# One unit of attention work made of 128 tokens from each of four sequences instead of 512 tokens in a row

## The chip, the core and the metric

One core of one Trainium2 chip runs the whole program. The metric is the device time of one execution in microseconds (us); lower is better. The engines are named as the profile names them: PE (matrix multiply), PEld (its weight load), DVE (vector), ACT (scalar), POOL (GpSimd) and SP, which issues the DMAs.

## What is computed

Three stages follow one another: a linear attention with a decaying state, and two feed-forward layers. Of the reference, what matters:

```python
B, H, S, D = 4, 8, 768, 48
state = zeros(B, H, D, D)
for t in range(S):
    state = alpha[:, :, t, :, None] * state + einsum('bhd,bhe->bhde', k[:, :, t], v[:, :, t])
    y[:, :, t] = einsum('bhd,bhde->bhe', q[:, :, t], state)
x = y.transpose(0, 2, 1, 3).reshape(3072, 384)
h = x @ w_in;  x = (h * cos(h)) @ w_out                      # d_ff 2048
h = max(x @ w1, x @ w2, x @ w3);  out = h @ w_out2           # d_ff 768
```

## The kernel before

**Tiling.** The 3072 tokens (four sequences of 768, one behind the other) are cut into NU = 6 units of HB = 512 tokens in a row, so a unit is two thirds of a sequence and a sequence begins at chunk 0 of units 0 and 3 and at chunk 4 of units 1 and 4. A unit has NC = 8 chunks of C = 64 tokens. The eight heads go in NP = 4 pairs; the pair's two heads lie on partitions 0 to 47 and 64 to 111 (PR = 112 rows). One call of `att` does one unit of one pair; there are 24 calls. All 24 are called attentions here, for short.

**One attention.** Two scans on DVE make the decays inside each chunk (`g`, L370 and L380) and their inverse form (`al`, L376 and L385). In the first unit a scan's second input lies in PSUM, in the later units in SBUF. Two POOL multiplies scale keys and queries (L372 or L384, and L387). PE transposes the keys (L392) and ACT copies them (L395). PE then multiplies keys with queries (L404) and keys with values (L409) into two PSUM banks `r`, one for even and one for odd chunks. The scores are masked into `a`: in the first unit by an ACT copy (L416) and a POOL multiply (L417), later by one DVE instruction (L420). The state goes through the unit's chunks one after the other on DVE: L428 computes state times decay plus the chunk's key-value product, on a 112x48 tile, once for each chunk; where a sequence begins L426 copies instead. The scaled states `d` that the queries need are made by POOL for all 8 chunks together (L440, one instruction for each of the pair's heads); in the first unit ACT makes those of one head, one chunk at a time (L435). PE then adds up the outputs in `values`: L453 multiplies scores with values in 64x64 tiles, and L459 multiplies scaled states with queries, two matmuls for each chunk on 112 rows and 48 columns; chunks that begin a sequence need none. `d` holds zeros outside the head's own rows, which the program writes once at the start (L638). ACT copies the output to the `xt` or `yy` tile (L474), and its low part follows (L477 and L479 in the first unit, L481 later).

**The layers.** `moe1` (L501 to L530) is the first layer: for each unit 16 blocks f, of which each needs 9 matmuls of 128x512 with `wi` (L501 to L503), an element-wise chain through `q` on ACT, DVE and POOL (L508 to L523), and 9 matmuls with `wo` (L528 to L530). Its weights come by DMA once, during the first unit: 32 blocks, each of which takes three DVE instructions (L315 to L317), an ACT copy (L320) and a POOL subtraction (L321). The second layer (L579 to L604) follows when the first has ended.

**What sets the order.** The order of all instructions is computed when the program is built: `Program.order` is a list scheduler with a duration for each operation, a due time, and a lag between engines; each engine then runs its own list in that order, in sequence. Operations marked `port=True` and all of POOL's are kept apart in the plan. PSUM has five shared banks, whose use the scheduler also assigns. Two engines that read one PSUM bank are put in the order in which the program states them.

## Time and profile before

| | |
|---|---|
| timed runs | 815.31, 817.70, 818.28 us; median 817.7 us |
| profiled execution, first to last instruction | 815.2 us, mean granted PE clock 0.985 |
| instructions | 15114 |
| PE busy | 791.5 us, 97% |
| DVE busy | 476.4 us, 58% |
| ACT busy | 360.9 us, 44% |
| POOL busy | 192.8 us, 24% |

The profiled execution's time outside its span is not given apart; its span lies 0.1 us under the lowest timed run and 2.5 us under the median. The shares are means over stages that differ: in the first 60 us all engines work on the first unit's attentions and on weights, from there to about 140 us the weights still arrive while the first unit's layer runs, and from then on PE alone is full. A busy share of PE says nothing on its clock: the granted clock stands beside it in the views by time. It was 1.00, full speed at 2.4 GHz, in most of the run, and 0.5, which is 1.2 GHz, in parts of the first 60 us.

### The profile page before, as it was taken

The page shows a single profiled execution, that of the slowest core. Times are in us where ns is not written, and L with a number is a line of the kernel's source. Part 1 is how long each engine was busy: PE and PEld are TensorE (multiplying, and loading weights), DVE is VectorE, ACT ScalarE, POOL GpSimd, SP SyncE. Part 2 cuts the span into 40 slices and gives each one's busy share as a digit, 9 for nine tenths or more (in the row PEclk, how much of TensorE's full clock was granted, in tenths as well). Part 3 has the DMA queues.
Part 4 walks back from the last instruction along what each step waited for, and adds up shares of the span by engine and source line. Part 5 has one row for each costly group of instructions (what it writes and reads, how often), then busy time and mean ns, then how long its engine had stood idle before and what let it go on. Part 6 is the DMA issues. An engine that isn't in the chain of part 4 may idle for free.

```text
span 815.2 us, 15114 instructions
## 1 busy us (share of the span) xinstructions
PE 791.5 (97%) x6168; PEld 646.0 (79%) x6168; DVE 476.4 (58%) x924; ACT 360.9 (44%) x667; POOL 192.8 (24%) x191
## 2 busy tenths in 40 slices
PE   7679999999999999999999999999999999999998
PEld 6567778888878878888888788888888888888886
DVE  7988999765786587667679955452232222322221
ACT  4575655555645565555577746531121121112121
POOL 7777876530231023101123200110000000000000
PEclk8789999999999999999999999999999999999999
DMA  9745564430242033103135600412020020200001
GB/s 273 214 132 174 182 209 141 130 93 5 88 147 54 2 115 108 43 1 108 34 107 161 221 23 1 156 58 86 26 83 27 14 91 26 78 27 13 14 27 39
DMA packets 26661, 71.86 MB, mean 88 GB/s; under 512 B 3488, under 2 KB 3488, under 8 KB 26592
## 3 DMA queue, kind: packets, MB, share of 16 engines
q1 hardware_dynamic: 26592, 70.90, 26.9%
q8 instruction: 48, 0.79, 0.4%
q14 instruction: 21, 0.17, 0.1%
HBM read 54.37 MB, written 14.16 MB: 84 GB/s over the span
## 4 chain that ended last, share of the span: by engine, by line
PE 84%; DVE 6%; POOL 4%; issue 2%; DMA 2%; ACT 2%; SPq 0%; POOLq 0%; DVEq 0%; ACTq 0%
PE ps L580 9%; PE ps L579 9%; PE ps L581 9%; PE acc L528 7%; PE ps L501 7%; PE acc L530 7%; PE acc L529 7%; PE ps L503 7%; PE ps L502 7%; PE ps L603 3%; PE ps L602 3%; PE ps L604 3%; PE ps L459 2%; PE ps L404 1%; PE ps L453 1%
## 5 line engine op out<-in xcount | busy, mean ns | idle before, releaser
L501 PE MATMUL ps<-xt,wih 128*128 128x512 f32 x288 | 116.3, 404 | 3.7 <-ACT kt L395 2.2
L528 PE MATMUL acc<-gh,woh 128*128 128x512 f32 x288 | 116.5, 405 | 0.7 <-DVE yy L538 0.5
L530 PE MATMUL acc<-gl,woh 128*128 128x512 f32 x288 | 112.8, 392 | 0.5 <-DVE gl L523 0.4
L502 PE MATMUL ps<-xt,wih 128*128 128x512 f32 x288 | 113.2, 393 | 0.0
L503 PE MATMUL ps<-xt,wil 128*128 128x512 f32 x288 | 113.0, 392 | 0.0
L529 PE MATMUL acc<-gh,wol 128*128 128x512 f32 x288 | 112.4, 390 | 0.0
L517 DVE SCALAR_TENSOR_TENSOR ps<-q,ps 128x512 f32<-128x512 f32 x76 | 52.7, 694 | 56.9 <-ACT q L511 56.7
L589 DVE TENSOR_TENSOR ps<-t,ps 128x512 f32<-128x512 f32 x36 | 25.0, 696 | 103.6 <-PE ps L581 103.5
L510 ACT ACTIVATE q<-q 128x512 f32<-128x512 f32 x96 | 60.5, 631 | 52.3 <-DVE q L509 52.0
L508 ACT ACTIVATE q<-ps 128x512 int32<-128x512 f32 x96 | 57.1, 595 | 57.0 <-PE ps L503 54.6
L509 DVE SCALAR_TENSOR_TENSOR q<-q,ps 128x512 f32<-128x512 int32 x96 | 65.7, 685 | 21.1 <-ACT q L508 20.8
L590 ACT ACTIVATE h<-ps 128x512 fp32r<-128x512 f32 x36 | 21.5, 598 | 112.1 <-DVE ps L589 112.0
L523 DVE TENSOR_TENSOR gl<-ps,gh 128x512 fp32r<-128x512 f32 x76 | 52.1, 686 | 26.7 <-PE ps L503 15.9
L501 PEld LDWEIGHTS ps<-xt,wih 128*128 128x128 f32 x288 | 54.7, 190 | 16.4 <-ACT kt L395 3.2
L440 POOL TENSOR_TENSOR d<-s,g 48x384 f32<-48x384 f32 x44 | 37.0, 842 | 125.5 <-DVE s L428 123.7
L587 DVE TENSOR_TENSOR t<-t,ps 128x512 f32<-128x512 f32 x36 | 24.8, 688 | 71.2 <-PE ps L581 70.4
L528 PEld LDWEIGHTS acc<-gh,woh 128*128 128x128 f32 x288 | 54.0, 188 | 14.9 <-DVE yy L538 2.3
L518 ACT ACTIVATE gh<-ps 128x512 fp32r<-128x512 f32 x76 | 45.4, 598 | 44.0 <-DVE ps L517 41.5
L530 PEld LDWEIGHTS acc<-gl,woh 128*128 128x128 f32 x288 | 54.1, 188 | 13.5 <-DVE gl L523 1.4
L503 PEld LDWEIGHTS ps<-xt,wil 128*128 128x128 f32 x288 | 54.7, 190 | 11.8
L502 PEld LDWEIGHTS ps<-xt,wih 128*128 128x128 f32 x288 | 54.9, 190 | 10.4
L529 PEld LDWEIGHTS acc<-gh,wol 128*128 128x128 f32 x288 | 54.1, 188 | 9.9
(122 smaller groups left out, 1579.4 us busy)
## 6 DMA issues: line engine op xcount, KB each, us to landing
raw<-in_wt SPq DMA_DIRECT2D x56, 384.0 KB, 3.3
kq<-in_qka SPq DMA_DIRECT2D x23, 448.0 KB, 4.2
x1d<-yy SPq DMA_DIRECT2D x18, 512.0 KB, 2.6
xt<-x1d SPq DMA_DIRECT2D x18, 512.0 KB, 4.4
v<-in_vv SPq DMA_DIRECT2D x22, 256.0 KB, 3.2
al<-in_qka SPq DMA_DIRECT2D x24, 228.4 KB, 2.7
outT<-y SPq DMA_DIRECT2D x18, 256.0 KB, 2.0
xt<-yy SPq DMA_DIRECT2D x36, 64.0 KB, 2.6
```

The source lines that it names most:

```text
L501: pe.matmul(ps, wi["h"][:, f, cc], xt[:, cc, 0], start=(cc == 0), stop=False)
L502: pe.matmul(ps, wi["h"][:, f, cc], xt[:, cc, 1], start=False, stop=False)
L503: pe.matmul(ps, wi["l"][:, f, cc], xt[:, cc, 0], start=False, stop=(cc == NR - 1))
L508: op("Act", act(HB, True), lambda: se.activation(q.bitcast(I32), ps, AF.Copy, scale=INV2PI), [hk], [qk], m)
L509: op("DVE", dve(HB), lambda: ve.scalar_tensor_tensor(q, q.bitcast(I32), -TWOPI, ps, ALU.mult, ALU.add), [hk], [qk], m)
L510: op("Act", act(HB), lambda: se.activation(q, q, AF.Sin, scale=0.5), (), [qk], m)
L528: pe.matmul(acc[c], oh, gh, start=(f == 0), stop=False)
L529: pe.matmul(acc[c], ol, gh, start=False, stop=False)
L530: pe.matmul(acc[c], oh, gl, start=False, stop=(f == NF1 - 1))
L579: pe.matmul(ps, w2t["h"][m][:, f, cc], xt[:, cc, 0], start=(cc == 0), stop=False)
L580: pe.matmul(ps, w2t["h"][m][:, f, cc], xt[:, cc, 1], start=False, stop=False)
L581: pe.matmul(ps, w2t["l"][m][:, f, cc], xt[:, cc, 0], start=False, stop=(cc == NR - 1))
```

## The change

A unit now holds 128 tokens of each of the four sequences, two chunks of each. The host arranges the inputs and the output for that; the arrays keep their shapes. Chunk c of a unit is chunk h = c % 2 of sequence i = c // 2, so the even bank of `r` holds all four sequences' first chunks and the odd bank all second ones. The state of a pair is one tile 112x(4x48) and takes two steps in a unit instead of eight. Every sequence begins in unit 0.

New names and lines (of the changed kernel): POOL multiplies the old states of all four sequences by the first chunk's decay into `d[:, 0]` (L421, not in unit 0); DVE adds the key-value products (L422), multiplies by the second chunk's decay into `d[:, 1]` (L423; in unit 0 L425 multiplies the key-value products straight from PSUM) and adds the second products (L430). `d` has no zeros any more. ACT copies half of the rows of each `d` into a new tile `z` (L428), whose other rows are zero from the start (L626). In `values` the matmul L446 takes the place of L459: in a first pass (x = 0) one head's 48 rows of `d` and of the queries alone, in a second (x = 1) the 112 rows of `z`. The old L426, L428, L435 and L440 are gone.

```diff
-    s_b = [ap.tile([PR, NC, D], F32, name=f"s{p}") for p in range(NP)]
-    d_b = [ap.tile([PR, 2, NC, D], F32, name=f"d{i}") for i in range(2)]
+    s_b = [ap.tile([PR, N2, D], F32, name=f"s{p}") for p in range(NP)]
+    d_b = [ap.tile([PR, 2, N2, D], F32, name=f"d{i}") for i in range(2)]
+    z_b = [ap.tile([PR, 2, N2, D], F32, name=f"z{i}") for i in range(2)]
...
-        for c in range(NC - 1):
-            op("DVE", 0.2, lambda c=c: state(c), [rk[c % 2], *kgs, (*sk, c)], [(*sk, c + 1)], t0 + 0.25)
...
+        kvs = [r[h][0:PR, 0:AO].rearrange("p (b e) -> p b e", b=N2) for h in range(2)]
+        gs = [g.rearrange("p (b h) t -> p b h t", h=2)[:, :, h, 0:1].to_broadcast([PR, N2, D]) for h in range(2)]
+        if u:
+            op("Pool", pool(N2 * D), lambda: ge.tensor_tensor(d[:, 0], s, gs[0], ALU.mult), [*kgs, sk], [(dk, 0)], t0 + 0.2)
+            op("DVE", dve(N2 * D), lambda: ve.tensor_tensor(s, kvs[0], d[:, 0], ALU.add), [rk[0], (dk, 0)], [sk], t0 + 0.25)
+            op("DVE", dve(N2 * D), lambda: ve.tensor_tensor(d[:, 1], s, gs[1], ALU.mult), [*kgs, sk], [(dk, 1)], t0 + 0.25, port=True)
+        else:
+            op("DVE", dve(N2 * D), lambda: ve.tensor_tensor(d[:, 1], kvs[0], gs[1], ALU.mult), [rk[0], *kgs], [(dk, 1)], t0 + 0.25)
+        for h in range(0 if u else 1, 2):
+            w = slice(UP * (1 - h), UP * (1 - h) + D)
+            op("Act", act(N2 * D), lambda h=h, w=w: se.activation(z[w, h], d[w, h], AF.Copy), [(dk, h)], [("z", n2, h)], t0 + 0.25)
+        if u + 1 < NU:
+            op("DVE", dve(N2 * D), lambda: ve.tensor_tensor(s, kvs[1], d[:, 1], ALU.add), [rk[1], (dk, 1)], [sk], t0 + 0.27)
...
-            for c in range(NC):
-                if not firsts[c]:
+            for x in range(2):
+                for i in range(N2):
                     for j in range(2):
-                        h = c % 2
-                        pe.matmul(y[h][UP * j:UP * j + D, c // 2 * C:(c // 2 + 1) * C], d[:, j, c], qv3[:, c], start=False, stop=False, skip_group_check=True)
...
+                        h, w = (j + x) % 2, slice(UP * j, UP * j + D)
+                        dd, qq = (z[:, h, i], qv3[:, 2 * i + h]) if x else (d[w, h, i], qv3[w, 2 * i + h])
+                        if u or h:
+                            pe.matmul(y[h][w, i * C:(i + 1) * C], dd, qq, start=False, stop=False, skip_group_check=True)
...
-            for t in (*s_b, *d_b):
+            for t in z_b:
                 ge.memset(t, 0.0)
```

The order of the lists moves with it, at three places that matter here.

DVE, first unit, before. The rows run from the third attention's last scan (`al_109`) through the state steps of the first two attentions (`s_125`, `s_122`) to the first weight block (`raw_92`) and the first step of the third attention (`s_123`):

```order
L376 SCALAR_TENSOR_TENSOR al_109<-al_109,acc_97 112x260
L426 COPY s_122<-ps_98 112x48
L428 SCALAR_TENSOR_TENSOR s_122<-s_122,g_114,ps_102 112x48
L428 SCALAR_TENSOR_TENSOR s_122<-s_122,g_114,ps_98 112x48
L428 SCALAR_TENSOR_TENSOR s_125<-s_125,g_113,ps_100 112x48
...
L315 TENSOR_SCALAR ps_99<-raw_92 128x384
L316 SCALAR_TENSOR_TENSOR ps_99<-raw_92,ps_99 128x384
L317 SCALAR_TENSOR_TENSOR raw_92<-raw_92,ps_99 128x384
L428 SCALAR_TENSOR_TENSOR s_122<-s_122,g_114,ps_102 112x48
L426 COPY s_123<-ps_100 112x48
```

The same engine and place in the changed kernel, where L371 is the scan and L311 to L313 are the weight block:

```order
L371 SCALAR_TENSOR_TENSOR al_109<-al_109,acc_97 112x260
L425 TENSOR_TENSOR d_126<-ps_101,g_115 112x192
L311 TENSOR_SCALAR ps_98<-raw_92 128x384
L430 TENSOR_TENSOR s_123<-ps_99,d_126 112x192
L312 SCALAR_TENSOR_TENSOR ps_98<-raw_92,ps_98 128x384
L313 SCALAR_TENSOR_TENSOR raw_92<-raw_92,ps_98 128x384
```

The third attention's state product now stands straight behind its last scan and ahead of the first weight block.

POOL, before, the work ahead of the first two `gl` (L515), which the first L528 needs; `kq_110` is the second unit's third attention, `d_126` its first, `wil` a weight block:

```order
L384 TENSOR_TENSOR kq_110<-kq_110,g_113 112x512
L440 TENSOR_TENSOR d_126<-s_125,g_114 48x384 x2
L387 TENSOR_TENSOR kq_110<-kq_110,al_107 112x512
L321 TENSOR_TENSOR wil<-raw_94,wih 128x384
L515 TENSOR_TENSOR gl_88<-q_83,gh_86 128x512
L515 TENSOR_TENSOR gl_89<-q_84,gh_87 128x512
```

And in the changed kernel (L379, L382 and L503 are the same operations as L384, L387 and L515):

```order
L379 TENSOR_TENSOR kq_110<-kq_110,g_113 112x512
L382 TENSOR_TENSOR kq_110<-kq_110,al_107 112x512
L421 TENSOR_TENSOR d_126<-s_123,g_113 112x192
L503 TENSOR_TENSOR gl_88<-q_83,gh_86 128x512
L503 TENSOR_TENSOR gl_89<-q_84,gh_87 128x512
```

No weight block stands right ahead of the first `gl` any more, and where two products of 48x384 for the first attention stood there is one of 112x192 for the third.

PE, one output block of a later unit, before (L453 the scores' part, L459 the states' part, L501 the layer's next matmul):

```order
L453 MATMUL ps_101<-a_120,v_116 64x64 x2
L453 MATMUL ps_99<-a_120,v_116 64x64 x2
L459 MATMUL ps_101<-kq_111,d_126 48x64 x2
L459 MATMUL ps_99<-kq_111,d_126 48x64 x2
...
L501 MATMUL ps_98<-xt_1844,wih 128x512
```

And in the changed kernel (L446 the states' part, first with `d`, then with `z`; L489 the layer's next matmul):

```order
L446 MATMUL ps_99<-kq_110,d_127 48x64
L446 MATMUL ps_100<-kq_110,d_127 48x64
...
L446 MATMUL ps_100<-kq_110,z_129 48x64
L446 MATMUL ps_99<-kq_110,z_129 48x64
...
L489 MATMUL ps_101<-xt_881,wih 128x512
```

There are 16 matmuls of L446 in each block of units 1 to 5, eight with `d`, whose successive matmuls change bank and rows each time, then eight with `z`; L459 had 16, or 14 where a sequence begins. In unit 0 L446 has eight.

## Rows read from the trace of the kernel before

**Rows 1.** The page, part 1: busy us of each engine; part 2: granted clock by slices

```profile
PE 791.5 (97%) x6168; PEld 646.0 (79%) x6168; DVE 476.4 (58%) x924; ACT 360.9 (44%) x667; POOL 192.8 (24%) x191
PEclk8789999999999999999999999999999999999999
```

**Rows 2.** Busy time by stretch: stretch, length, PE, PEld, DVE, ACT, POOL, clock, DMA

```profile
0.00:20.00 20.00, 15.28 (x298) 13.91 (x298) 15.64 (x43) 9.12 (x26) 15.57 (x27) 0.83 0.94 273
20.00:40.00 20.00, 14.01 (x264) 11.11 (x263) 17.90 (x42) 11.64 (x35) 15.44 (x15) 0.75 0.72 216
40.00:60.00 20.00, 15.26 (x168) 11.95 (x169) 17.35 (x37) 13.28 (x26) 15.53 (x14) 0.83 0.40 128
60.00:80.00 20.00, 19.67 (x173) 14.97 (x173) 17.98 (x41) 11.87 (x24) 14.84 (x13) 1.00 0.60 187
80.00:100.00 20.00, 18.82 (x224) 15.41 (x219) 19.28 (x43) 13.01 (x27) 18.04 (x15) 1.00 0.57 175
100.00:120.00 20.00, 18.02 (x195) 13.95 (x193) 19.88 (x44) 12.04 (x25) 15.95 (x14) 1.00 0.63 195
200.00:400.00 200.00, 200.00 (x2102) 162.00 (x2094) 141.18 (x286) 112.47 (x201) 39.60 (x40) 1.00 0.23 71
```

**Rows 3.** Timeline of PE, three places: start us, us, instruction; the group count of L459

```profile
164.41 0.69 PE L404 MATMUL ps<-kq 48*64 48x64 f32 x32
164.93 0.62 PE L409 MATMUL ps<-v,kt 64*64 64x48 f32 x32
...
207.40 0.69 PE L453 MATMUL ps<-a,v 64*64 64x64 f32 x32
208.03 0.99 PE L459 MATMUL ps<-kq,d 112*48 112x64 f32 x28
208.95 0.50 PE L501 MATMUL ps<-xt,wih 128*128 128x512 f32 x1
...
161.11 1.10 PE L459 MATMUL ps<-kq,d 112*48 112x64 f32 x32
162.14 0.50 PE L501 MATMUL ps<-xt,wih 128*128 128x512 f32 x1
...
L459 PE MATMUL ps<-kq,d 112*48 112x64 f32 x592 | 20.7, 222 | 0.0
```

**Rows 4.** Groups by line; the first two of 10.3 to 49 and 49 to 130 us

```profile
L428 DVE SCALAR_TENSOR_TENSOR s<-s,g,ps 112x48 f32<-112x48 f32 x34 | 8.5, 255 | 1.7 <-ACT a L416 1.4
L428 DVE SCALAR_TENSOR_TENSOR s<-s,g,ps 112x48 f32<-112x48 f32 x29 | 7.5, 257 | 0.2
L420 DVE TENSOR_TENSOR a<-ps,tri 128x256 f32<-128x256 f32 x40 | 15.4, 417 | 3.0 <-PE ps L409 3.0
L435 ACT ACTIVATE d<-s,g 48x48 f32<-48x48 f32 x28 | 9.0, 332 | 2.1 <-DVE s L428 1.4 <-DVE s L426 0.4
L474 ACT ACTIVATE xt<-ps 128x256 fp32r<-128x256 f32 x30 | 10.3, 377 | 7.3 <-PE ps L459 7.2
```

**Rows 5.** Timeline of DVE and PE in the first 60 us, single rows

```profile
14.33 0.69 DVE L376 TENSOR_TENSOR_SCAN al<-al,acc 112x260 f32<-112x260 f32 x1
17.40 0.56 DVE L315 TENSOR_SCALAR ps<-raw 128x384 uint32<-128x384 uint32 x1 [0.36 <-DMA raw<-in_wt]
18.84 0.97 PE L409 MATMUL ps<-q,kt 64*64 64x48 f32 x32
48.95 0.69 DVE L509 SCALAR_TENSOR_TENSOR q<-q,ps 128x512 f32<-128x512 int32 x1 [0.30 <-ACT q L508]
59.88 0.50 PE L528 MATMUL acc<-gh,woh 128*128 128x512 f32 x1
```

**Rows 6.** One line's instructions: shortest, median, longest ns; POOL's products as a group

```profile
L385 DVE TENSOR_TENSOR_SCAN al<-al,inv x20: 1227/1241/2422, 35.7 to 367.5; 112x520 f32<-112x520 f32 x20
L387 POOL TENSOR_TENSOR kq<-kq,al x23: 1173/1194/2102, 6.8 to 373.8; 112x512 f32<-112x512 f32 x23
L440 POOL TENSOR_TENSOR d<-s,g 48x384 f32<-48x384 f32 x44 | 37.0, 842 | 125.5 <-DVE s L428 123.7
```

More of the change, by code (lines that the diff above doesn't have):

```diff
@@ L359, in att @@
         kg, ik, tk, dk, sk = ("g", m % NGS), ("iv", n2), ("kt", n2), ("d", n2), ("s", p)
-        firsts = [(u * NC + c) % CPB == 0 for c in range(NC)]
         op("SP", HW, lambda: nc.sync.dma_start(t, qka[u, p, :, 0:KO]), (), [kf], t0 - 4, dma(PR * KO * 4))
@@ L421, in att @@
                    [rk[j], "tri"], [("a", n2, j)], t0 + 0.2)
-        def state(c):
-            o, kvc = s[:, (c + 1) % NC], r[c % 2][0:PR, c // 2 * D:(c // 2 + 1) * D]
-            if firsts[c]:
-                ve.tensor_copy(o, kvc)
-            else:
-                ve.scalar_tensor_tensor(o, s[:, c], g[:, c, 0:1], kvc, ALU.mult, ALU.add)
-        for c in range(NC - 1):
-            op("DVE", 0.2, lambda c=c: state(c), [rk[c % 2], *kgs, (*sk, c)], [(*sk, c + 1)], t0 + 0.25)
-            if u < DAC and not firsts[c + 1]:
-                for j in range(DAH):
-                    w = slice(UP * j, UP * j + D)
-                    op("Act", act(D) + 0.21, lambda c=c, j=j, w=w: se.activation(d[w, j, c + 1], s[w, c + 1], AF.Copy, scale=g[w, c + 1, 0:1]),
-                       [*kgs, (*sk, c + 1)], [(dk, j, c + 1)], t0 + 0.25)
@@ L437, in att @@
-        for j in range(2):
-            if u >= DAC or j >= DAH:
-                w = slice(UP * j, UP * j + D)
-                op("Pool", pool(NC * D), lambda j=j, w=w: ge.tensor_tensor(d[w, j], s[w], g[w, :, 0:1].to_broadcast([D, NC, D]), ALU.mult),
-                   [*kgs, *[(*sk, c) for c in range(NC)]], [(dk, j, c) for c in range(NC)], t0 + 0.25)
-            elif not firsts[0]:
-                w = slice(UP * j, UP * j + D)
-                op("Act", act(D) + 0.21, lambda j=j, w=w: se.activation(d[w, j, 0], s[w, 0], AF.Copy, scale=g[w, 0, 0:1]), [*kgs, (*sk, 0)], [(dk, j, 0)], t0 + 0.25)
@@ L709, in heads @@
     def heads(a):
[L711 to L712 removed]
+        a = _np.asarray(a).reshape(B, NP, 2, NU, 2, C, D)
+        return a.transpose(3, 1, 2, 6, 0, 4, 5).reshape(NU, NP, 2, D, NC, C)
     al, q, k = heads(inputs["alpha"]), heads(inputs["q"]), heads(inputs["k"])
```

21 lines of the change are left out of this document (8 added, 13 removed).

## The prediction

> **What bounds the kernel now.** I read the page first: PE is busy 97% of the span [rows 1], so the question is where the last 3% lie and what PE's own work costs. The busy time by stretch answers the first half. From 200 to 400 us PE is busy all the time while DVE is at 71% and POOL at 20%: there only PE's own work counts, and nothing that DVE, ACT or POOL save is seen in the end [rows 2]. In the first 60 us PE is busy 44.6 of 60 us (15.28 + 14.01 + 15.26), at a granted clock of 0.75 to 0.83, while DVE and POOL are busy 78 to 90% of each 20 us; from 60 to 120 us PE loses another 3.5 us (60 - 19.67 - 18.82 - 18.02) with DVE at 90 to 99% [rows 2]. So the change can act in three places: on PE's attention blocks everywhere, on the start, and a little in the 60 us behind it. The start ends, for this purpose, when PE's first L528 runs, at 59.88 us; from there PE is nearly full [rows 2, 5].
>
> **PE's output blocks.** Starts in the steady stretch give a block's price. The scores' part L453 takes 208.03 - 207.40 = 0.63 us, the states' part L459 with 28 records 208.95 - 208.03 = 0.92 us, with 32 records 162.14 - 161.11 = 1.03 us [rows 3]. Four records more cost 0.11 us, so a record on 112 rows costs 0.0275 us, and 0.92 - 28 x 0.0275 = 0.15 us is fixed. The score block L404, also 32 records but in tiles of 64x64, takes 164.93 - 164.41 = 0.52 us, 0.016 us a record: in these tiles two matmuls run side by side [rows 3]. The trace has two records for each of these matmuls. 592 records in 20 blocks mean that 12 have 28 and 8 have 32 [rows 3].
>
> After the change a block of units 1 to 5 has 16 records on 48 rows, whose successive matmuls use opposite corners of the array and different banks, and 16 records on 112 rows. If the corners run side by side as in L404, the first half costs 16 x 0.016 = 0.26 us and the second 0.15 + 16 x 0.0275 = 0.59 us, together 0.85 us. That is 0.07 us less than a block of 28 and 0.18 us less than one of 32: 12 x 0.07 + 8 x 0.18 = 2.3 us, all of it on the path, since PE is full there. The trace shows neither such corners nor such a pair; the bounds are L404 at one end and L459's record price at the other. By the latter the first half costs 16 x 0.0275 = 0.44 us, the block 1.03 us, and the 12 short blocks lose 0.11 us each: 1.3 us more instead of 2.3 us less. I take the side nearer to L404, because rows and banks of the two corners differ as they do there. The rows say one thing more: L404 is followed by L409, whose tiles lie otherwise in the array, without a gap (0.52 us for 32 records), while L453 of the same size takes 0.63 us before L459 on 112 rows; the step to 112 rows costs about 0.11 us, and there is one such step before and after. The Trainium skill (TensorEngine Tiling (Array Packing), Key Properties) states that a change of tiling mode, unlike a change of tile, drains TensorE; the step of 0.11 us agrees with it. If 64x64 to 48x48 counted as such a change too, it would cost 20 x 0.11 = 2.2 us and take the gain away; L404 to L409 speaks against that.
>
> In unit 0 a block falls from 28 records to 16. PE waits there anyway, so this is part of the start and not counted again.
>
> **DVE.** One state step costs 0.26 us [rows 4], eight of them 2.05 us an attention. The new instructions have 192 columns. Between 48 columns at 0.257 us and 256 at 0.417 us [rows 4] a line gives 0.26 + 144 x 0.00077 = 0.37 us; three make 1.1 us in units 1 to 5, two make 0.74 us in unit 0. Until the first L509 at 48.95 us DVE does 34 steps and 5 copies of the same length now, 39 x 0.25 = 9.7 us [rows 4, 5]; afterwards 8 + 3 instructions, 4.1 us. So 5.6 us of DVE are freed in the start. From 49 to 130 us there are 29 steps and 3 copies, the equal of four attentions, and 8.2 us become 4.4: 3.8 us freed. All later savings lie under a full PE and count nothing.
>
> **Where the start's 5.6 us go.** I followed the new order through with durations of the trace. DVE ends the third attention's scans near 15.2 us (now 14.33 + 0.69 = 15.02 [rows 5]). Next in its list stands the third attention's product, which needs that attention's L409. L409 ends at 19.8 now [rows 5]; in the new order PE does the first attention's output about 2 us earlier, because the masks end then, but then waits for POOL's L387 of the third attention and for its own slow clock, so I find 18.9. DVE stands about 3.7 us. Before, those 3.7 us held eight state steps and a weight block, whose DMA had landed by 17.40 [rows 5]. Later two scans of unit 1 come to lie beside POOL's multiplies. L385 takes 1.24 us alone and up to 2.42, L387 1.19 and up to 2.10 [rows 6]: one stands while the other works. I count 1.2 us twice. 5.6 - 3.7 - 2.4 = -0.5: at the first L509 the new kernel is no earlier than the old.
>
> Behind it POOL is shorter: six products of 0.84 us [rows 6] stand before the first L515 now, three afterwards of half the columns; between nothing (they fit into idle time) and 6 x 0.84 - 3 x 0.45 = 3.7 us comes of that. The weight block ahead of the first L515 is gone too, and PE's list has two groups of three layer matmuls fewer, but one more score block, ahead of the first L528. Followed through, it runs at about 57.5 instead of 59.88 us: 2.4 us gained. ACT's new copies (112x192 source, half the rows; between 0.33 and 0.38 us [rows 4]) replace 28 short ones in unit 0, which frees 9.0 - 4 x 0.35 = 7.6 us of an engine that doesn't bound here; two in each later attention lie under PE.
>
> From 60 to 120 us PE loses 3.5 us beside a DVE that is freed of 3.8 us. Weights arrive just in time there, so a start 2.4 us earlier uses part of that; I take 1.5 us, between 0 and 3.5.
>
> **The sum.** 2.3 + 2.4 + 1.5 = 6.2 us. The profiled execution's span is 815.2 us, 2.5 us under the median of the timed runs; 815.2 - 6.2 = 809.0, and against the median 817.7 - 6.2 = 811.5 us.
>
> **The rivals.**
> - *The freed time shows in full.* If the DVE list's wait for the third attention is covered and the scans meet POOL at other points, 5.6 + 3.8 + 2.3 = 11.7 us are gained: 806.0 us. For it: DVE is the busiest engine beside PE from 20 to 120 us. Against: the order puts the wait there, and PE loses only 3.5 us behind the start.
> - *The start stands still.* The chain through POOL's multiplies, ACT and the DMA into `xt` decides, and only PE's blocks gain: 817.7 - 2.3 = 815.4 us.
> - *The corners don't run side by side* (the change then doesn't do all that it may): the sum loses 2.3 + 1.3 = 3.6 us: 815.1 us.
> - *Slower, by a lock.* The new product L423 reads two SBUF tiles, as L385 does, where L428 read one and PSUM. If each of unit 1's four waits for a POOL multiply (1.2 us [rows 6]) and five scans more do so (1.2 us each), and the weights, one block later (3 x 0.56 = 1.7 us [rows 5]), hold PE from 60 to 120 us, 4.8 + 6.0 + 1.7 = 12.5 us stand against 3.8 and 2.3: 6.4 us more, 824.1 us. It decides from 10.2 us of such waits on (2.3 + 3.8 + 4.1 for half a per cent). For it are the long rows of L385 and L387; against it that POOL is busy only 20% where most of L423 stand [rows 2]. The Trainium skill (SBUF — State Buffer, Who interferes with whom) states that a DVE instruction with two SBUF inputs and a GpSimd one that reads SBUF shut each other out for the whole instruction. The long rows agree; by that rule alone this rival would be the outcome only if nearly every pair met.
>
> **How the numbers follow.** A measurement of this kernel can tell about 0.5%, 4.1 us, from no change. Forecast 811.5 us: 0.45. Freed time in full, 806.0: 0.18. Start stands still, 815.4: 0.20. No side by side, 815.1: 0.09. Slower, 824.1: 0.08. The forecast's own spread is about 2.5 us either way (0 to 3.7 us from POOL, 0 to 3.5 us behind the start); about a fifth of it lies above 813.6. So faster 0.18 + 0.37 + 0.03 from the upper two cases = 0.58, within 0.5% 0.34, slower 0.08. The range goes from 805.0, under the second case, to 817.5, which holds the two cases at 815 and leaves out the slower one.
>
> **What would show it.** In the new profile: two successive starts of output blocks 0.85 us apart (1.03 if the corners are serial); three DVE instructions of 112x192 at 0.35 to 0.4 us an attention, L423 longer beside POOL; DVE idle for 3 to 4 us near 15 to 19 us, ended by PE; the first L516 (old L528) near 57.5 us; a full PE from 130 us on. Wrong I would be by a first L516 later than 60 us or by PE losing more than 3.5 us from 60 to 120 us.

## The result, and the profile after

The changed kernel takes 823.8 us (median of 822.96 to 825.28) beside 818.0 us of the kernel before on the same chip: a ratio of 1.0079, 95% interval 1.0059 to 1.0098. It is slower, where 811.5 us was forecast with a range that ended at 817.5. The profiled execution took 822.96 us with a span of 821.3 us; before it was 815.2.

The page of the changed kernel, span, busy times and clock, answers to [rows 1]:

```profile
span 821.3 us, 14946 instructions
PE 794.8 (97%) x6168; PEld 646.5 (79%) x6168; DVE 460.8 (56%) x796; ACT 369.1 (45%) x683; POOL 162.5 (20%) x163
PEclk9599999999999999999999999999999999999999
```

DVE has 128 instructions and 15.6 us less, POOL 30 us less, ACT 8 us more: the change does what it says. PE is busy 3.3 us longer (794.8 against 791.5) and idle 2.8 us longer (821.3 - 794.8 = 26.5 against 23.7). Together this is the 6.1 us of the span. Of the 3.3 us, 1.3 are PE's output blocks (below) and about 1.7 a lower clock in 125 to 135 us. Busy time by stretch of the changed kernel (stretch, length, PE, PEld, DVE, ACT, POOL, clock, DMA share, GB/s), answering to [rows 2]:

```profile
0.00:20.00 20.00, 15.55 (x335) 14.19 (x335) 13.78 (x32) 7.61 (x20) 12.77 (x23) 0.91 0.93 268
20.00:40.00 20.00, 14.39 (x177) 11.01 (x178) 17.45 (x32) 7.55 (x19) 13.81 (x13) 0.57 0.80 214
40.00:60.00 20.00, 15.93 (x246) 12.04 (x245) 15.96 (x33) 13.81 (x29) 13.50 (x13) 0.91 0.59 177
60.00:80.00 20.00, 19.77 (x203) 15.84 (x202) 19.78 (x35) 11.15 (x23) 13.78 (x12) 1.00 0.56 169
80.00:100.00 20.00, 19.25 (x253) 14.81 (x252) 19.93 (x40) 13.46 (x29) 14.53 (x14) 1.00 0.67 194
100.00:120.00 20.00, 19.28 (x202) 15.00 (x201) 18.98 (x38) 13.84 (x28) 14.13 (x14) 1.00 0.60 180
120.00:140.00 20.00, 15.58 (x176) 12.01 (x175) 19.22 (x35) 8.99 (x18) 14.47 (x12) 0.91 0.40 121
400.00:500.00 100.00, 97.48 (x540) 78.36 (x539) 72.92 (x129) 62.20 (x111) 18.53 (x18) 1.00 0.32 104
```

The kernel before, in two of these stretches that [rows 2] leaves out:

```profile
120.00:140.00 20.00, 20.00 (x263) 16.41 (x263) 19.75 (x45) 9.86 (x19) 12.90 (x12) 1.00 0.49 152
400.00:500.00 100.00, 98.95 (x546) 80.03 (x545) 75.73 (x137) 63.80 (x115) 20.18 (x20) 1.00 0.32 104
```

Up to 120 us PE is busy 3.1 us more than before, about what the forecast's second and third terms (3.9 us) promised. (Busy times of the first 60 us compare here, since the granted clock has the same mean of 0.80 there in both kernels.) Then one stretch spoils it: from 120 to 140 us PE is busy 15.58 of 20 us at a clock of 0.91, where it had been full (20.00) before. In 400 to 500 us another 1.5 us go (97.48 against 98.95). DVE, though freed of work, is as full from 60 to 140 us as before.

The hole in single rows of the changed kernel: PE's waits, then DVE's list, then the ACT instruction between them (start us, us, instruction, idle before it and what ended that):

```profile
126.90 0.50 PE L516 MATMUL acc<-gh,woh 128*128 128x512 f32 x1 [1.34 <-ACT gh L502]
128.31 0.79 PE L518 MATMUL acc<-gl,woh 128*128 128x512 f32 x1 [0.68 <-POOL gl L503]
128.90 0.63 PE L516 MATMUL acc<-gh,woh 128*128 128x512 f32 x1
139.77 0.50 PE L489 MATMUL ps<-xt,wih 128*128 128x512 f32 x1 [2.40 <-DVE raw L313]
...
132.42 2.68 DVE L375 TENSOR_TENSOR_SCAN g<-al,one 112x520 f32<-112x520 f32 x2
136.31 2.37 DVE L380 TENSOR_TENSOR_SCAN al<-al,inv 112x520 f32<-112x520 f32 x2
138.59 0.66 DVE L497 SCALAR_TENSOR_TENSOR q<-q,ps 128x512 f32<-128x512 int32 x1
139.17 0.55 DVE L313 SCALAR_TENSOR_TENSOR raw<-raw,ps 128x384 uint32<-128x384 uint32 x1
...
139.28 0.63 ACT L498 ACTIVATE q<-q 128x512 f32<-128x512 f32 x1 [4.97 <-DVE q L497]
```

Two waits of the layer's chain come first, and behind them the matmuls take 0.63 us instead of 0.39 for some 2.5 us: PE runs at the lower of its two levels, 1.2 GHz, there (granted clock 0.80 in 125 to 130 us and 0.86 in 130 to 135, together 1.7 us short of the full clock). Then four scans stand on DVE in front of L497, whose operand is ready at 134.3 us and which runs at 138.59; between them lies a half-done weight block, whose last instruction L313 runs at 139.17 and gives up the PSUM bank that PE waits 2.40 us for. Before the change the scans of this stretch stood singly, at 124.00, 132.09 and 137.22 us, with layer, weight or state instructions between them.

That is where most of the time is lost. Why is another question: these scans are one of several things in the planner's new order, and the runs had to separate the order from the operations.

### The profile page after: what moved, and what is told of

The parts are those of the page before. It is cut to its first block, busy times and chain, and to the rows that moved or that the text cites. A ratio compares the mean times of both kernels' runs of the same rounds, so it can differ in the third digit from the quotient of the medians.

```text
span 821.3 us, 14946 instructions
## 1 busy us (share of the span) xinstructions
PE 794.8 (97%) x6168; PEld 646.5 (79%) x6168; DVE 460.8 (56%) x796; ACT 369.1 (45%) x683; POOL 162.5 (20%) x163
## 4 chain that ended last, share of the span: by engine, by line
PE 78%; DVE 10%; issue 4%; DMA 3%; POOL 2%; ACT 2%; SPq 0%; DVEq 0%; POOLq 0%; ACTq 0%
PE ps L567 9%; PE ps L568 9%; PE ps L569 9%; PE ps L489 6%; PE acc L516 6%; PE ps L491 6%; PE ps L490 6%; PE acc L518 6%; PE acc L517 6%; PE ps L591 3%; PE ps L590 3%; PE ps L592 3%; PE ps L446 2%; PE ps L399 2%; DVE ps L312 2%
## 5 line engine op out<-in xcount | busy, mean ns | idle before, releaser
L489 PE MATMUL ps<-xt,wih 128*128 128x512 f32 x288 | 117.6, 408 | 3.4 <-DVE raw L313 2.4
L516 PE MATMUL acc<-gh,woh 128*128 128x512 f32 x288 | 115.5, 401 | 1.6 <-ACT gh L502 1.3
L498 ACT ACTIVATE q<-q 128x512 f32<-128x512 f32 x96 | 60.6, 632 | 65.0 <-DVE q L497 64.5
L497 DVE SCALAR_TENSOR_TENSOR q<-q,ps 128x512 f32<-128x512 int32 x96 | 65.4, 683 | 22.3 <-ACT q L496 21.8
L511 DVE TENSOR_TENSOR gl<-ps,gh 128x512 fp32r<-128x512 f32 x76 | 52.2, 687 | 33.9 <-ACT gh L506 17.3
L489 PEld LDWEIGHTS ps<-xt,wih 128*128 128x128 f32 x288 | 54.8, 190 | 15.9 <-DVE raw L313 2.8
L516 PEld LDWEIGHTS acc<-gh,woh 128*128 128x128 f32 x288 | 54.3, 189 | 15.0 <-ACT gh L502 1.9
L575 DVE TENSOR_TENSOR t<-t,ps 128x512 f32<-128x512 f32 x36 | 24.8, 688 | 70.4 <-PE ps L569 69.7
L499 ACT ACTIVATE q<-q 128x512 f32<-128x512 f32 x96 | 60.5, 630 | 2.6
```

Of the source, the lines that this page charges most:

```text
L489: pe.matmul(ps, wi["h"][:, f, cc], xt[:, cc, 0], start=(cc == 0), stop=False)
L497: op("DVE", dve(HB), lambda: ve.scalar_tensor_tensor(q, q.bitcast(I32), -TWOPI, ps, ALU.mult, ALU.add), [hk], [qk], m)
L498: op("Act", act(HB), lambda: se.activation(q, q, AF.Sin, scale=0.5), (), [qk], m)
L499: op("Act", act(HB), lambda: se.activation(q, q, AF.Square), (), [qk], m)
L516: pe.matmul(acc[c], oh, gh, start=(f == 0), stop=False)
```

## The experiments

### One number of the planner, and both kernels

The planner works out one order for all engines from costs and due times. A different number gives the same instructions in another order. In the planner's own reckoning the changed kernel's order contains a hole: TensorE stands 2.80 us at 119 us and is then reckoned slow for a while. So the same change was tried under other orders, and the kernel before as well.

```
-    return 0.07 + 0.00104 * n      (fixed cost of a DVE instruction)
+    return 0.08 + 0.00104 * n
```

> The changed kernel with one number of the planner altered: its fixed cost of a DVE instruction is 0.08 us instead of 0.07. All instructions stay, only their order from about 50 us on is another. In the planner's own reckoning the order of the changed kernel has TensorE standing 2.80 us at about 119 us, and slowed for 7 us behind it, and this order has no such hole. Theory A (the order is what costs): the stretch 120 to 140 us shows TensorE busy 19 us or more instead of 15.58, and the time is 815 to 820. Theory B (the operations cost): 822 to 825, with the lost time somewhere else between 60 and 200 us.

> The kernel before with the planner's fixed cost of a DVE instruction at 0.08 us, the same number that took the changed kernel from 823.8 to 816.9 us. Only the order of its instructions changes. In the planner's own reckoning it ends at 814.0 us as it does with 0.07. Theory A (the order decides, and the change by itself is worth little): 816 to 820, so that under this number the changed kernel is equal or ahead. Theory B (the change costs some 6 us under any order, and 0.08 is simply the better number for both kernels): 809 to 813.

```
-MOE_EARLY = 4
+MOE_EARLY = 2
```

> The changed kernel with another number of the planner: MOE_EARLY is 2 instead of 4, which makes the layer's elementwise instructions two units less urgent against weights and scans. The planner's own reckoning ends at 809.7 us, with no hole over 1.4 us behind 60 us. Theory A (order): with the 6.5 us that separate the reckoning from the measurement in the two orders of this kernel so far (817.3 and 823.8, 810.4 and 816.9), 814 to 818. Theory B (operations): 821 to 825.

> The kernel before with MOE_EARLY 2; its reckoning ends at 810.9 us instead of 814.0. Theory A (order): the measurement follows the reckoning, 813 to 817, and the changed kernel with the same number lies within 2 us of it. Theory B (operations): the changed kernel with the same number is at least 3 us slower than this one.

```
-MOE_EARLY = 4 / ATT0 = -3.0 / ATTS = 2.5
+MOE_EARLY = 2 / ATT0 = -2.0 / ATTS = 2.75
```

> The changed kernel with three numbers of the planner altered: MOE_EARLY 2, the attentions of later units due one step later (ATT0 -2 instead of -3) and spread further (ATTS 2.75 instead of 2.5). The reckoning ends at 808.8 us, the least among those of single numbers that were worked out. Theory A (order): 813 to 817, no wait of TensorE over 1.5 us between 120 and 145 us. Theory B (operations): 821 or more.

> The kernel before with the three planner numbers of the changed kernel's best order (MOE_EARLY 2, ATT0 -2, ATTS 2.75), the fourth pair of orders in which both kernels have been run. In its own reckoning it ends at 817.3 us, the changed kernel at 808.8. Theory A (each kernel has its own lucky orders, and a pair under the same numbers says little): 818 to 823. Theory B (these numbers are good for either kernel): 813 to 816. Over the four pairs the changed kernel less the kernel before is then, in the order of the runs, about +6, 0, +2.5 and, by A, -2 to -7.

Measured, each as a ratio to the kernel before on the same chip, with its interval:

| planner's numbers | kernel before | changed kernel | difference |
|---|---|---|---|
| as given | 1 (818.0 us) | 1.0079 (1.0059 to 1.0098), 823.8 us | +0.79% |
| DVE cost 0.08 | 0.9991 (0.9976 to 1.0005), 816.6 us | 0.9992 (0.9978 to 1.0007), 816.9 us | 0 |
| MOE_EARLY 2 | 0.9976 (0.9962 to 0.9990), 815.0 us | 1.0000 (0.998 to 1.002), 817.5 us | +0.24% |
| MOE_EARLY 2, ATT0 -2, ATTS 2.75 | 1.0023 (1.0005 to 1.0040), 818.8 us | 0.9988 (0.9972 to 1.0003), 816.0 us | -0.35% |

The runs e2, e5, e6, e8 and e17 came out as their theory A; e7 fits neither of its two, since its partner is 2.5 us slower, more than 2 and less than 3. The order moves the changed kernel by 7 to 8 us, and the kernel before by nearly 4. With the 0.08 the hole is gone, in this row of that run:

```profile
120.00:140.00 20.00, 19.60 (x200) 15.24 (x200) 19.31 (x37) 12.50 (x25) 12.44 (x11) 1.00 0.61 179
```

PE is busy 19.60 us there beside a DVE that is as full as in the slow order (19.31 and 19.22). So it is not how much DVE does in this stretch but what it does first. Theory A held for the loss; but no pair shows the gain of 6 us that was forecast: the mean of the four differences is +0.17%, 1.4 us, with a spread far larger than that.

A rule instead of a number, on the same idea: DVE doesn't begin far-off work when something more urgent is about to become ready.

```
...
+            if e == "DVE":
+                soon = [j for j in waiting[e] if t < ready(j) < t + 0.8 * self.ops[i][1]
+                        and self.ops[j][5] + 6 < self.ops[i][5]]
+                if soon:
+                    free[e] = min(map(ready, soon))
+                    continue
```

> The changed kernel with one rule added to its planner: DVE doesn't begin a piece of work that is due more than six units after another piece which becomes ready before four fifths of the first would be done; it waits for the more urgent one. All costs and due times stay. In the planner's reckoning it ends at 809.1 us instead of 817.3. Theory A (the greedy order puts far-off scans and weight pieces in front of L497 and L501, and that is what costs): 814 to 818, TensorE busy 19 us or more in 120 to 140 us. Theory B (the change's operations): 821 to 825. A third possibility, that any disturbance of the order gives the same 816 whatever its sense, is not told apart from A by this run.

818.1 us, ratio 1.0003 (0.9985 to 1.0020), with PE busy 19.80 us in 120 to 140 us: 5.7 us come back, no more than with an arbitrary other number. As expected, this doesn't tell a good rule from any disturbance of a bad order.

### Moving work within the bad order

The first edit moves two of the scans with what hangs on them; the lines that keep one weight block's instructions together are left out here.

```
+    move([late[3, 0], late[3, 0, 1], late[3, 0, 2], late[3, 0, 3], late[3, 0, 4]], late[2, 2, "s"])
```

> The changed kernel (823.8 us) with the same instructions and the same planned order, except that at 126 to 135 us the two scans L375 and L380 of unit 3's first attention, with the reciprocal and the two GpSimd products behind them, stand behind the last state update of unit 2's third attention (some 15 us later in the plan), and that one weight block's three DVE instructions stand together instead of having scans and a layer instruction between them. Theory A (the order that the planner now finds is what costs: it puts four scans in a row on DVE ahead of L497, whose operand had been ready 4.97 us, and splits a weight block, whose PSUM bank TensorE then waits 2.40 us for): these scans take 1.34 + 0.19 + 1.18 = 2.7 us out of the way of L497, the wait for the bank at 139.8 us goes, and the time falls by 2 to 4 us, to 820 to 822. Theory B (the change's own operations cost: the lock of L423, the slower output block, the longer chain d, z, output): nothing of that is touched, 823 to 825.

828.5 us, 1.0144 (1.0121 to 1.0167): worse by 4.6 us, a miss. The wait for the bank at 140 us shrinks only from 2.40 to 1.1 us, since the two scans that stay are longer beside POOL (1.55 and 2.09 us instead of 1.34 and 1.19), and where the moved ones land, scans bunch again: three stand ahead of L497 and a fourth ahead of L526. DVE of that run:

```profile
154.92 2.08 DVE L380 TENSOR_TENSOR_SCAN al<-al,inv 112x520 f32<-112x520 f32 x1
156.93 1.21 DVE L375 TENSOR_TENSOR_SCAN g<-al,one 112x520 f32<-112x520 f32 x1
158.06 0.66 DVE L497 SCALAR_TENSOR_TENSOR q<-q,ps 128x512 f32<-128x512 int32 x1
```

and its wait of PE for the L526 that stands behind them (in total, times, longest):

```profile
PE acc L516 <- DVE yy L526: 3.0, 1, 3.0
```

The run shows the mechanism at a second place, though not the remedy: scans bunched ahead of the layer's instructions make PE wait there too, 3.0 us this time.

The second edit puts three weight blocks of the second layer elsewhere in the order; the loop that moves them is left out.

```
+    places = [(first[NW1 + n], order[at]) for n, at in enumerate((912, 940, 971))]
```

> The changed kernel in its own order, except that the three weight blocks of the second layer whose nine DVE instructions stand at 123 to 140 us are put at 184, 193 and 202 us, where DVE is some 60% busy; nobody uses them before 290 us. Theory A (in 120 to 140 us far-off work on DVE stands in front of the layer's instructions): nine instructions of 0.47 us from start to start, 4.2 us, leave this stretch, the weight block whose PSUM bank TensorE waits 2.40 us for is no longer there, and 3 to 5 us come back: 819 to 821. Theory B (the order there is of no account): 823 to 825.

824.9 us, 1.0087 (1.0059 to 1.0114): nothing comes back, a second miss. DVE of that run:

```profile
131.17 4.16 DVE L375 TENSOR_TENSOR_SCAN g<-al,one 112x520 f32<-112x520 f32 x2
135.49 3.06 DVE L380 TENSOR_TENSOR_SCAN al<-al,inv 112x520 f32<-112x520 f32 x2
138.47 0.66 DVE L497 SCALAR_TENSOR_TENSOR q<-q,ps 128x512 f32<-128x512 int32 x1
```

The scans begin 1.25 us earlier, since weight pieces ahead of them and between them are gone, and L497 runs at 138.47 instead of 138.59. The pairs take 4.16 and 3.06 us where they took 2.68 and 2.37: started earlier, they meet POOL's L503, which takes 2.19 us instead of 1.30 and for which PE then waits 1.14 us, ahead of L379, which they met before as well. What was freed on DVE was eaten by the two engines holding each other up.

### Single operations of the change

Both passes of the state part on 112 rows, so that the 48-row shape is gone (the cut shows PE's part; ScalarE makes two padded copies where it made one):

```
-                        dd, qq = (z[:, h, i], qv3[:, 2 * i + h]) if x else (d[w, h, i], qv3[w, 2 * i + h])
+                        dd, qq = z[:, h, j, i], qv3[:, 2 * i + h]
```

> The changed kernel with both passes of the state part of the output block on 112 rows: ScalarE makes padded copies of both halves (two activations where one stood, in the same place of the order), and no 48-row matmul is left. Theory A on the block: the 48-row records run two abreast, 27.5 ns apart, exactly as the 112-row ones, so that nothing is gained by them, and the step of 146 ns between the two shapes is pure loss: L438 and L446 together go from 1.658 to about 1.54 us, 20 blocks give 2.3 us, and the time is 820.5 to 822.5. Theory B: the 48-row pass is cheaper or dearer by itself (then the block comes out over 1.60 or under 1.48 us), or the longer chain through ScalarE (0.36 us more for each state half) costs what TensorE gains: 823 or more.

826.3 us, 1.0114 (1.0094 to 1.0133). A block of this run, and one of the changed kernel in the steady stretch, with one of its unit 0:

```profile
209.39 0.69 PE L442 MATMUL ps<-a,v 64*64 64x64 f32 x32
210.02 1.10 PE L450 MATMUL ps<-kq,z 112*48 112x64 f32 x32
211.05 0.50 PE L493 MATMUL ps<-xt,wih 128*128 128x512 f32 x1
```

```profile
206.38 0.69 PE L438 MATMUL ps<-a,v 64*64 64x64 f32 x32
206.89 0.63 PE L446 MATMUL ps<-kq,d 48*48 48x64 f32 x16
207.45 0.65 PE L446 MATMUL ps<-kq,z 112*48 112x64 f32 x16
208.04 0.50 PE L489 MATMUL ps<-xt,wih 128*128 128x512 f32 x1
...
18.38 0.61 PE L446 MATMUL acc<-kq,d 48*48 48x64 f32 x8
18.92 0.65 PE L446 MATMUL acc<-kq,z 112*48 112x64 f32 x8
```

From L442 or L438 to the layer's next matmul both take 1.66 us. I had expected 1.54: the step to the 112-row shape is not saved, it only moves ahead of the whole state part (0.63 us for L442 against 0.51 for L438). The Trainium skill (TensorEngine Tiling (Array Packing), Key Properties) states that a change of tiling mode drains the engine; that agrees with the 0.12 us that stays in the block wherever the one change stands. So the 48-row pass costs just as much as a 112-row one. The 2.4 us that this run takes more lie in the same hole: between 120 and 145 us PE's waits come to 6.4 us, where they are 4.4 in the changed kernel. That ScalarE's added copies make them longer is likely and not shown.

The product that reads two SBUF tiles, on GpSimd instead of DVE (L423 alone; L425 of unit 0 stays on DVE, other than the expectation says):

```
-lambda: ve.tensor_tensor(d[:, 1], s, gs[1], ALU.mult)
+lambda: ge.tensor_tensor(d[:, 1], s, gs[1], ALU.mult)
```

> The changed kernel with the product L423 (L425 in unit 0) on GpSimd instead of DVE, at the same place of the planned order. DVE loses 20 instructions of 0.35 us and the 2.5 us by which L423 was longer beside GpSimd; GpSimd gets 20 of about 0.5 us. Theory A (order): neither is what sets the time, 822.5 to 825. Theory B (the operations, above all DVE and GpSimd holding each other up at L423): 2 us or more come back, 819 to 822.

822.5 us, 1.0070 (1.0046 to 1.0095), within the interval of the changed kernel: theory A. In its first order the time that DVE and GpSimd hold each other up at this product is not what sets the time.

What DVE time is worth under a fixed order:

```
...
+                for o in (spare, spare, s):
+                    ve.tensor_tensor(o, kvs[1], d[:, 1], ALU.add)
...
```

> The changed kernel in the order that takes 816.9 us (fixed DVE cost 0.08), with two more DVE instructions of 0.33 us beside each state update L430 of units 0 to 4 (20 times, 13 us of DVE time, about what the change freed), which write the same sum to a spare tile; the order is planned without them. Theory A1 (DVE time that is freed is worth nothing here, since the planner fills it with work that isn't yet needed): 816 to 818.5. Theory A2 (under a fixed order DVE time is worth its full length in 60 to 140 us, where DVE is over 95% busy and 7 of the 20 places lie): 5 us more, 820 to 823; then the freed time was worth something and the order took it away.

824.7 us, 1.0078 (1.0053 to 1.0104), against 816.9 without the 13 us of DVE work: 7.8 us more, above the range of theory A2. Counted along PE's 512-column matmuls, the same order in both runs, 4.9 us of delay are there by the 31st (54 us in the faster run), 8.2 by the 251st (123 us), 8.9 at 154 us, and from there to the end 0.3 more. In the start a single wait grew from 1.5 us to

```profile
PE ps L388 <- DVE d L426: 4.5, 1, 4.5
```

By 154 us 11 of the 20 places have run, 7.3 us of added DVE time. So DVE time is worth its length and somewhat more where PE isn't full, and next to nothing behind 150 us. Not all of the delay is waiting: the clock granted in the first three stretches of 20 us is lower too, 0.78, 0.67 and 0.67 where the faster run has 1.00, 0.76 and 0.81. Under a fixed order DVE time is worth something; the next runs show how much of it the new operations give back.

### The new operations in the old order

Here the planner plans with the state operations of before, and the new operations take their places; all other instructions stand as in the kernel before. (The planning part, shortened.) Where exactly the new ones stand among the old places was chosen once, by hand; another choice was not run.

```
+        if planned is None:
+            for c in range(NC - 1):
+                op("DVE", 0.2, None, [...], [(*sk, c + 1)], t0 + 0.25, tag=("st", u, k, c))
...
+    place = [planned[t] if t in planned else planned[t[:-1]] + t[-1] for t in tags]
+    order = sorted(range(len(tags)), key=lambda i: place[i])
```

> The changed kernel's operations in the order of the kernel before: the planner works out its order with the state operations of before (which are not issued), and the new operations take their places. The product L421 on GpSimd stands right behind the state matmuls L404 of its attention, the sum L422 where the first state update stood, the product L423 at the second, the last sum L430 at the eighth, the padded copies on ScalarE at the first update and at the second of the old GpSimd products. All other instructions stand exactly as in the kernel before. Theory A (the operations are worth what the prediction's second and third steps said, and the planner's new order loses it): 818.0 - 2.4 - 1.5 + 1.4 (output blocks as measured) = 815.5, so 814 to 817. Theory B (the operations themselves give nothing under any order): 817.5 to 819.5. Theory C (they cost): 820 or more.

> The same with the order that the kernel before has under MOE_EARLY 2, in which that kernel takes 815.0 us. Theory A: 2.5 us less, 811 to 814, and the least of all the orders. Theory B: 814.5 to 816.5. Theory C: 817 or more. If e12 and this one stand the same way to their partners, the worth of the operations is told apart from the luck of an order; if they differ by more than 2 us, even in a given order the worth depends on which order it is.

821.4 us, 1.0045 (1.0025 to 1.0065), and 819.2 us, 1.0018 (1.0001 to 1.0036), where the partner of the second has 0.9976: 0.45% and 0.42% slower, in two orders alike: theory C both times. Along the 512-column matmuls the first of them is 0.6 us late at 55 us, 1.6 at 66, 4.0 at 108, 3.8 from 154 to 207, and 4.7 at the end. Places can be read directly, since all other instructions stand in the same order. First the start, DVE of the run in the old order:

```profile
13.00 0.69 DVE L372 TENSOR_TENSOR_SCAN al<-al,acc 112x260 f32<-112x260 f32 x1
14.12 0.35 DVE L445 TENSOR_TENSOR s<-ps,d 112x192 f32<-112x192 f32 x1
17.25 0.56 DVE L312 TENSOR_SCALAR ps<-raw 128x384 uint32<-128x384 uint32 x1 [2.79 <-DMA raw<-in_wt]
```

DVE is done with its scans 1.33 us earlier than before (13.00 against 14.33 [rows 5]) and has finished the states 2.6 us earlier (14.47 against 17.04), but the weight block behind them starts at 17.25 instead of 17.40: it waits for its DMA, 2.79 us now, 0.36 us before [rows 5]. Nothing of the freed time comes through.

Then 67 to 72 us, the kernel before and the run in the old order:

```profile
67.56 0.55 DVE L428 SCALAR_TENSOR_TENSOR s<-s,g,ps 112x48 f32<-112x48 f32 x2
68.03 1.23 DVE L385 TENSOR_TENSOR_SCAN al<-al,inv 112x520 f32<-112x520 f32 x1
69.18 0.54 DVE L315 TENSOR_SCALAR ps<-raw 128x384 uint32<-128x384 uint32 x1
69.63 0.25 DVE L428 SCALAR_TENSOR_TENSOR s<-s,g,ps 112x48 f32<-112x48 f32 x1
69.80 0.56 DVE L316 SCALAR_TENSOR_TENSOR ps<-raw,ps 128x384 uint32<-128x384 uint32 x1
```

```profile
67.88 0.35 DVE L437 TENSOR_TENSOR s<-ps,d 112x192 f32<-112x192 f32 x1
68.26 0.94 DVE L438 TENSOR_TENSOR d<-s,g 112x192 f32<-112x192 f32 x1
69.13 2.06 DVE L381 TENSOR_TENSOR_SCAN al<-al,inv 112x520 f32<-112x520 f32 x1
```

Two old steps stood ahead of the scan; now a sum and the product do, the product takes 0.94 us beside POOL instead of 0.36, and the scan behind it, which then meets POOL's L380, 2.06 instead of 1.23. An old step keeps DVE only 0.17 us from its own start to the next instruction's (69.63 to 69.80), since successive instructions overlap; its own duration is 0.25.

PE doesn't lose time here, though (1.6 us late at 66 us, 2.0 at 93). It loses it at two other places. Between 55 and 60 us it is full in both runs, and the granted clock is 0.53 where it was 0.78. And near 100 us, in the run in the old order:

```profile
100.33 0.91 PE L454 MATMUL ps<-a,v 64*64 64x64 f32 x32 [1.83 <-DVE raw L314]
103.05 0.80 PE L531 MATMUL acc<-gh,woh 128*128 128x512 f32 x1
```

PE waits 1.83 us for a bank that a weight piece gives up, where the kernel before waits 0.45 and 0.73; DVE has come to that piece 2.3 us later than before (99.72 against 97.40). Behind the wait PE runs at its lower level: the block takes 2.72 us instead of 1.66, and the granted clock is 0.66 in 100 to 105 us, where it was 1.00. In the second old order PE idles 3.8 us between 55 and 140 us, and 1.05 in its partner.

```
-lambda: ve.tensor_tensor(d[:, 1], s, gs[1], ALU.mult)      (in the old order)
+lambda: ge.tensor_tensor(d[:, 1], s, gs[1], ALU.mult)
```

> The changed operations in the order of the kernel before (821.4 us), with the product L438 (L423 of the changed kernel) on GpSimd instead of DVE, in the same place. In that run L438 took 0.43 to 1.02 us in the five places between 40 and 130 us where it took 0.36 alone, 1.9 us more, and the old-order run fell 3.3 us behind the kernel before between 40 and 125 us. Theory L (what the operations cost is this product, held up beside GpSimd): DVE gets back 5 x 0.36 + 1.9 = 3.7 us of which two thirds count, and the time is 818 to 819.8. Theory M (the rest of the new chain, GpSimd's product ahead of the sums and the padded copies, costs as much on its way): 820.5 to 823.

821.5 us, 1.0042 (1.0027 to 1.0057): by the median nothing, as theory M had it. Its times go from 819.2 to 822.0; the profiled execution, at 819.2 the shortest, is 0.35 us late at 108 us where the other was 4.0, and there the clock near 100 us stays full after a wait of 1.33 us. How much of the cost is DVE and GpSimd holding each other up at this product stays open by this pair.

### The product on GpSimd in better orders

The same edit on two of the orders above:

> The changed kernel in its best order so far (815.95 us, MOE_EARLY 2, ATT0 -2, ATTS 2.75) with the product L423 on GpSimd. Theory L: 1 to 2.5 us less, 813.5 to 815, ahead of both kernels. Theory M: 815.5 to 818.

> The changed kernel in the order with the fixed DVE cost 0.08 (816.9 us), with the product L423 on GpSimd. Theory L: 814.5 to 816. Theory M: 816.5 to 819. With the first order (823.8 and 822.5 with the product on GpSimd) and the two others of this set it shows whether the product's place is worth the same under every order.

813.8 us, 0.9962 (0.9947 to 0.9978), and 816.5 us, 0.9984 (0.9967 to 1.0001). The first is ahead of the changed kernel by some 10 us and of the kernel before by 0.38%; against the kernel before in its own better order (0.9976) the intervals overlap. The edit gave 0.26% in one order, as theory L had it, and 0.08% in the other, between its two; in both the intervals of the runs with and without it overlap.

## Why the prediction was wrong, point by point

**Which steps failed.** Two of them. The sum took the output blocks at 2.3 us gained, and they cost 1.3. And it had no term for the stretch behind 120 us, where it expected a full PE: 4.4 us of waits, about 1.7 of lower clock and 1.5 in 400 to 500 us were lost there. The gain up to 120 us, forecast 3.9 us, came at 3.1. With these, 1.3 + 4.4 + 1.7 + 1.5 - 3.1 = 5.8 of the 6.1 us of span are accounted for.

**PE's output blocks.** Forecast 2.3 us less, measured 1.3 us more: 12 blocks of the kernel before took 0.63 + 0.92 = 1.55 us from the first matmul of the score part to the layer's next and 8 took 1.66 us [rows 3]; all 20 now take 1.66 us, so 12 x 0.11 are lost. That is the forecast's own other bound, but for another reason than the "serial" it gave. In unit 0 one corner alone takes 0.54 us for 8 records (18.38 to 18.92); in the steady stretch two corners take 0.56 us for 16 (206.89 to 207.45), each with the step to the next shape. They do run side by side, and a pair of corners is then as fast as a pair of 112-row matmuls. The 0.016 us a record that I took over from L404 [rows 3] belongs to four corners at once, and the rate had been carried to a pattern that has only two. That L404 has "two matmuls side by side", as the prediction says, was the misreading: the program's loop there goes over both row halves and both column halves, so it has four.

**The start.** Forecast: first L516 at 57.5 us, DVE waiting 3 to 4 us near 15 to 19 us for PE. Measured in the changed kernel:

```profile
18.17 0.36 DVE L425 TENSOR_TENSOR d<-ps,g 112x192 f32<-112x192 f32 x1 [2.50 <-PE ps L404]
57.32 0.50 PE L516 MATMUL acc<-gh,woh 128*128 128x512 f32 x1
```

The first L516 came out, and the wait for PE at 2.50 us. Why the start gained is only in part shown. The forecast reckoned DVE's freed time as used up there and put the 2.4 us down to POOL's shorter work and PE's list. In the old order POOL's work is shorter too, and the same matmul runs at 61.47 us instead of 59.88: the operations alone bring the start nothing, so the gain is the new order's. Which part of that order it is, no run separates; the number was hit without its reason being shown. For the old order the row at 17.40 [rows 5] already said why DVE's freed time is lost: its wait was ended by the DMA, 0.36 us after DVE had come free. I read the DMA as landed and not as the bound that the freed time would run into.

**60 to 120 us.** Forecast 1.5 us gained, measured 1.8 (PE loses 1.70 instead of 3.49 us). But the forecast named "a full PE from 130 us on" as its sign, and PE lost 4.4 us in 120 to 140 us. Neither of its two signs of being wrong showed, since both looked no further than 120 us. The prediction followed the new order through to 60 us and stopped; of the 80 us behind it, with DVE over 95% full, 60 were given a number without being followed and the last 20 none, and the order there is what made the result. Under the other three planner orders the changed kernel lies between 0.9988 and 1.0000.

**DVE's saving was mis-sized.** Forecast 2.05 - 1.1 = 0.95 us an attention. DVE's busy time fell by 15.6 us in 24 attentions, 0.65 us each: a step's duration (0.255 us [rows 4]) was counted in full though another instruction behind it starts 0.17 us after it (69.63 to 69.80 above), and 2.3 us went to longer rows of L423. By themselves the new instructions were sized rightly, by these rows of DVE in the changed kernel (shortest, median, longest ns):

```profile
L430 DVE TENSOR_TENSOR s<-ps,d x20: 343/350/358, 11.5 to 328.2; 112x192 f32<-112x192 f32 x20
L423 DVE TENSOR_TENSOR d<-s,g x20: 345/358/1260, 43.7 to 406.7; 112x192 f32<-112x192 f32 x20
```

**The rival that came nearest.** "Slower by a lock" gave 824.1 us, and 823.8 was measured, but not by its sum. L423 is 2.3 us over its median in all 20 places together, not 4.8 in four; the forty scans of 112x520 together stand 4.7 us over 1.23 us each, where they stood 2.8 before, so 1.9 us more and not 6.0; and taking the product off DVE returned 0.03 to 0.26% under four orders (1.0079 to 1.0070, 1.0045 to 1.0042, 0.9992 to 0.9984, 0.9988 to 0.9962). The Trainium skill (SBUF — State Buffer, Who interferes with whom) states that such a product and a GpSimd instruction that reads SBUF exclude each other; the rows with 0.94 and 1.26 us agree, and the scans at 2.06 us do too. What it costs depends on the order in which they meet.

**What the 5.8 us are, then.** In the order that the planner gave, mostly the stretch from 120 to 140 us. The 1.5 us in 400 to 500 us are waits too: PE waits 0.84 us for L511 at 429 us, and for the bank of a weight piece ahead of a matmul of the second layer, where the kernel before waits 0.51 and 0.36 us:

```profile
472.53 0.50 PE L567 MATMUL ps<-xt,w1h 128*128 128x512 f32 x1 [1.28 <-DVE raw L313]
```

Under two given orders the new operations cost 0.42 to 0.45%, some 3.5 us: 1.3 of it PE's blocks, the rest waits and, in the first of them, a lower clock near 58 and 102 us. That the waits come of DVE and GpSimd holding each other up is argued from the rows at 67 to 72 us and not shown, since taking the product off DVE left the median where it was. An order planned for the operations gives back more or less than this: in the planner's four, the difference to the kernel before runs from +6.5 to -2.9 us, and the given numbers hit the worst. An order without the hole returns no more because the gain goes again further on. With the 0.08, in this row, PE is busy 3.5 us more up to 120 us than in the kernel before (101.07 us, at a clock of 0.90):

```profile
0.00:120.00 120.00, 104.54 (x1405) 83.20 (x1406) 108.04 (x207) 67.64 (x142) 90.30 (x89) 0.93 0.70 200
```

It then loses 0.4 us in 120 to 140 us, 0.6 in 400 to 500 and the blocks' 1.3, which leaves about the 0.9 us by which its span is shorter (814.3 against 815.2). What of the new order brings the early gain stays open.

## What to carry to other kernels

Where a greedy planner sets the order, a change of operations is two changes; try both versions under a few planner numbers before either is judged, for here one version moved by nearly 8 us without a changed instruction. Freed engine time is worth something only if the next instruction in that engine's list was waiting for nothing else: look at what ended the idle time in front of it. A rate per record holds for the number of array corners that were busy when it was read. And a forecast that follows an order has to follow it as far as the engines are full, or say that it stops.

## What the hardware showed that was not expected

- Small matmuls, from start to start of their records: 0.055 us a record with one corner of the array in use (48 rows, unit 0), 0.0275 with two, 0.016 with four (L404); on 112 rows and 48 columns 0.0275, two of them side by side.
- Short DVE instructions overlap: a state step of 0.255 us holds up an instruction other than the next step by 0.17 us (seven steps on end take 1.81 us, 0.26 each), and behind a weight piece of 0.55 us the next instruction starts 0.47 us after it, by the median. The sum of durations overstates what removing instructions frees: 48.7 us of old state instructions gave way to 24.8 us of new ones, and DVE's busy time fell by 15.6.
- The same two scans took 2.68 us in the changed kernel and 4.16 us when they started 1.25 us earlier against the same GpSimd list.
